# The mask of a fused attention and feed-forward kernel moved from VectorE to ScalarE, and its order planned anew

## The chip, the cores and the metric

The kernel runs on one core of a Trainium2 chip. Its engines are TensorE (PE in the rows; PEld is its loading of stationary operands), VectorE (DVE), ScalarE (ACT) and GpSimd (POOL); SyncE (SP) issues every DMA. The time is device microseconds of one execution; the figure for a kernel is the median of its runs.

## What is computed

Attention over 4 batch entries of 8 heads, 576 positions and 64 dimensions, in which each row keeps only the scores within `tau` of its largest one; then two feed-forward parts on the 2304 tokens.

```python
scores = q @ k.T / 8
thresh = max(scores, axis=-1) - tau
scores = where(scores >= thresh, scores, -1e9)
attn = exp(scores - max(scores)); attn /= sum(attn) + 1e-9
x = attn @ v                                  # to (2304, 512)
x = ((x @ w1) * (x @ w2)) @ w3 @ w_out        # 512 -> 1024 -> 1024 -> 512
h = x @ w_in; out = (h * sigmoid(h)) @ w_out2  # 512 -> 2048 -> 512
```

## The kernel before

Every float32 operand of a product is split into a high and a low part of the narrower type that TensorE takes, and a product is made of three passes (high by high, high by low, low by high). The feed-forward weights arrive as 64-bit words. For the first batch entry they are turned into float32 in SBUF, by one ScalarE instruction ("w scale", line 931) and three VectorE instructions ("w shift", "w sign", "w low", lines 938, 945 and 953), and written back to DRAM; the later entries load the float32 copy.

Attention is done in tiles of 128 query rows, 36 for a batch entry and 144 in all. For each tile (function `qtiles`) TensorE writes the scores to one of two PSUM buffers `s` (line 677). VectorE takes the row maximum, negated, into a free column of that buffer ("max", line 653), and makes two small vectors from it ("bias", lines 661 and 667): the bias of exp, and the threshold. ScalarE takes exp of the scores from PSUM into an SBUF buffer `e` (line 704). VectorE reads the scores a second time, compares them with the threshold, multiplies `e` by the result and accumulates the row sums ("mask", line 714); with it the buffer `s` is done. ScalarE scales the sums, VectorE takes the reciprocal, and the probabilities become pairs of fp16: the high part on ScalarE (line 747), the low part on VectorE (line 754) or, for some tiles, on GpSimd. A transposing DMA brings them to `pt`, and TensorE multiplies them with the values (line 818).

The program has stages. Stage 0 is the attention of the first batch entry together with the product of `w3` and `w_out` (called W34, line 1022). Each of the four stages that follow is the feed-forward part of one batch entry (line 976, function `product`, 1344 matmuls in each stage) merged with the attention of the next. All products take turns on two PSUM buffers `m`. Each one is emptied by ScalarE first (a copy at line 401, a tanh at line 1090, or half of an output at line 1113) and in most cases by VectorE after it (lines 1059 and 1097).

The order on each engine is not written by hand. `Plan` records every operation with an expected duration, and `Plan.run` makes a list schedule: at each step it takes the operation that can start first by the expected times, and among equals the one with the least priority. A priority is the place in the merged program plus a shift from the table `BIAS`, by kind of operation and phase. In the schedule before, VectorE and GpSimd do not know of each other. The schedule is made while the program is built; on the chip each engine runs its instructions in the order written.

Of the kernel before, what the change touches and what calls it, by code (L numbers as in the profile page):

```python
# [30 lines left out]
BIAS = [  # L31
    {
        "1/sum": -468, "bias": -68, "consts": 57, "exp": -44, "kh": -81, "kl": -76, "mask": -267,
        "max": 18, "p": 155, "p hi": -98, "p lo": 55, "pv": -15, "qh": -23, "qk load": -40,
        "ql": 28, "scores": -62, "sum": 3, "tau load": 69, "turn": 40, "v load": 22,
# [3 lines left out]
    },  # L39
    {  # L40
        "w low": 288, "w scale": 37, "w shift": -86, "w sign": -12, "w34": -80, "w34 keep": -68,
        "w34 out": 165, "w64 load": -100,
    },
    {
        "w low": 1206, "w scale": -64, "w shift": -69, "w sign": -25, "w34": 51, "w34 keep": -63,
        "w34 out": -84, "w64 load": -57,
    },
    {
# [7 lines left out]
    },  # L56
    {
        "1/sum": 41, "bias": -22, "exp": 14, "g": -12, "kh": -98, "kl": 30, "mask": -9, "max": 30,
        "p": -62, "p hi": -52, "p lo": 17, "product": -29, "pv": -172, "qh": 34, "qk load": -68,
        "ql": 5, "scores": -60, "split hi": 104, "split lo": -55, "sum": -24, "tanh": 8,  # L60
# [46 lines left out]
    },  # L107
    {
        "a": -22, "ab": -17, "g": -27, "o": 34, "o half": -92, "out": -97, "product": 29,
        "split hi": 21, "split lo": -20, "tanh": 88, "w hi": -36, "w lo": 38, "w load": -11,  # L110
        "y hi": -85, "y lo": -13,
    },
]
# [1156 lines left out]
```

## Time and profile before

| What | Value |
|---|---|
| Runs (3) | 1053.49, 1053.56, 1053.84 us |
| Median | 1053.56 us |
| Profiled execution, span from first to last instruction | 1052.6 us |
| Mean granted TensorE clock | 0.992 of full speed |
| Busy PE, DVE, ACT, POOL | 974.8, 678.1, 640.4, 558.1 us |
| DMA | 175.26 MB, 65.1% of 16 engines' span |

The profiled execution is known by its span; the median of the runs is 0.96 us above it. Busy time of an engine is the time in which at least one of its instructions runs. It is an average over stages that differ, so it is read by stage. The ends of matmuls are modelled, so PE's busy time holds some waiting. ACT and DVE start an instruction a little before the last one has ended; the cost of one in a dense stretch is therefore the distance from start to start.

### The profile page before, as it was taken

How to read it: one execution, taken by the hardware profiler on the slowest of the kernel's cores; microseconds unless marked ns; L12 is line 12 of the kernel's file. 1: busy time of each engine (PE TensorE's matmuls, PEld its weight loads, DVE VectorE, ACT ScalarE, POOL GpSimd, SP SyncE). 2: the span in 40 equal slices, each digit the busy share in tenths (PEclk: the TensorE clock that was granted, in tenths of full speed). 3: DMA queues.
4: the chain of work that ended last, by engine and by line, in shares of the span. 5: the costliest groups of instructions: out<-in, count | busy, mean ns of one | idle time of the engine just before them, and what ended most of it. 6: DMA issues, size and time to landing. Idle time of an engine off the chain costs nothing.

```text
span 1052.6 us, 18100 instructions
## 1 busy us (share of the span) xinstructions
PE 974.8 (93%) x6832; PEld 900.7 (86%) x6832; DVE 678.1 (64%) x1334; ACT 640.4 (61%) x980; POOL 558.1 (53%) x305
## 2 busy tenths in 40 slices
PE   3479988999888989999999999999999999999998
PEld 2345556999888888999899999999999999999998
DVE  7999899997999999873881756656477221112021
ACT  6677777777675867764774756655676523324350
POOL 3343434666384574465475673754663735646472
PEclk9989999999999999999999999999999999999999
DMA  7899989995798979856753739465466332222221
GB/s 213 211 247 242 243 193 269 278 278 129 208 254 204 264 202 249 196 134 134 161 148 106 163 114 210 138 152 134 128 121 159 102 113 92 80 81 81 81 81 66
DMA packets 213368, 175.26 MB, mean 166 GB/s; under 512 B 175264, under 2 KB 179360, under 8 KB 213280
## 3 DMA queue, kind: packets, MB, share of 16 engines
q1 hardware_dynamic: 213280, 174.10, 65.1%
q8 instruction: 54, 0.88, 0.3%
q14 instruction: 34, 0.28, 0.1%
HBM read 112.20 MB, written 19.40 MB: 125 GB/s over the span
## 4 chain that ended last, share of the span: by engine, by line
PE 55%; DVE 21%; DMA 11%; ACT 6%; issue 6%; SPq 1%; POOL 1%; ACTq 0%; DVEq 0%; POOLq 0%
PE m L976 45%; DMA pt<-hl 4%; PE m L818 4%; PE s L677 4%; DVE hl L754 3%; DVE s L653 3%; DVE e L714 2%; DVE wr L953 2%; PE m L1022 2%; DMA w<-wr 2%; DVE wr L945 2%; DMA qk<-qkv 1%; ACT hl L747 1%; DVE tb L1097 1%; DMA vr<-qkv 1%
## 5 line engine op out<-in xcount | busy, mean ns | idle before, releaser
L976 PE MATMUL m<-act,hi 128*128 128x288 f32 x2560 | 450.7, 298 | 13.5 <-DVE tb L1097 7.9
L976 PEld LDWEIGHTS m<-act,hi 128*128 128x128 f32 x2560 | 375.1, 189 | 19.4 <-DVE tb L1097 9.3
L420 POOL TENSOR_TENSOR lo<-wr,hi 128x1024 fp32r<-128x1024 f32 x102 | 249.5, 2447 | 227.5 <-PE m L976 131.3
L976 PE MATMUL m<-act,lo 128*128 128x288 f32 x1280 | 274.0, 296 | 0.0
L976 PEld LDWEIGHTS m<-act,lo 128*128 128x128 f32 x1280 | 206.0, 189 | 0.0
L401 ACT ACTIVATE hi<-wr 128x1024 fp32r<-128x1024 f32 x112 | 118.4, 1057 | 116.5 <-PE m L976 82.1
L976 PE MATMUL m<-x,hi 128*128 128x288 f32 x1024 | 179.7, 297 | 3.9 <-DVE x L847 1.2
L420 POOL TENSOR_TENSOR act<-tb,act 128x576 fp32r<-128x576 f32 x96 | 151.3, 1582 | 43.4 <-ACT act L401 28.9
L976 PEld LDWEIGHTS m<-x,hi 128*128 128x128 f32 x1024 | 150.2, 189 | 6.9 <-DVE x L847 2.1
L754 DVE SCALAR_TENSOR_TENSOR hl<-e,st,hl 128x576 f16<-128x576 f32 x117 | 126.5, 1095 | 33.4 <-ACT hl L747 33.0
L704 ACT ACTIVATE e<-s,st,sc 128x576 f32<-128x576 f32 x144 | 118.5, 826 | 46.4 <-DVE hl L754 16.2
L714 DVE SCALAR_TENSOR_TENSOR e<-s,st,e 128x576 f32<-128x576 f32 x144 | 115.5, 810 | 14.3 <-ACT e L704 12.6
L653 DVE TENSOR_REDUCE s<-s 128x1 f32<-128x576 f32 x144 | 108.0, 756 | 24.7 <-PE s L677 24.6
L677 PE MATMUL s<-kh,qs 128*128 128x288 f32 x320 | 81.6, 338 | 44.5 <-DVE e L714 25.7
L1097 DVE SCALAR_TENSOR_TENSOR tb<-ta,m 128x576 f32<-128x576 f32 x64 | 48.0, 750 | 104.0 <-ACT ta L1090 99.9
L976 PE MATMUL m<-x,lo 128*128 128x288 f32 x512 | 109.5, 295 | 0.0
L677 PEld LDWEIGHTS s<-kh,qs 128*128 128x128 f32 x320 | 54.6, 202 | 61.5 <-issue 41.2
L747 ACT ACTIVATE hl<-e,st 128x576 f16<-128x576 f32 x117 | 87.8, 768 | 28.2 <-DVE st L727 14.2
L818 PE MATMUL m<-pt,vst 128*128 128x288 f16 x656 | 99.9, 296 | 5.0 <-DMA pt<-hl 2.8
L818 PEld LDWEIGHTS <-vst 128*128 128x128 f16 x656 | 60.5, 101 | 32.3 <-issue 8.8
L420 POOL TENSOR_TENSOR qs<-qk,qs 64x576 fp32r<-64x576 f32 x31 | 49.3, 1590 | 69.9 <-ACT qs L508 55.3
L401 ACT ACTIVATE act<-tb 128x576 fp32r<-128x576 f32 x96 | 65.4, 682 | 29.9 <-DVE tb L1097 25.4
(69 smaller groups left out, 1073.5 us busy)
## 6 DMA issues: line engine op xcount, KB each, us to landing
wr<-w SPq DMA_DIRECT2D x88, 512.0 KB, 3.4
qk<-qkv SPq DMA_DIRECT2D x31, 576.0 KB, 4.8
r<-wo SPq DMA_DIRECT2D x24, 512.0 KB, 6.1
w<-wr SPq DMA_DIRECT2D x24, 512.0 KB, 4.7
vr<-qkv SPq DMA_DIRECT2D x16, 576.0 KB, 4.2
r<-w3t SPq DMA_DIRECT2D x16, 512.0 KB, 5.6
r<-w SPq DMA_DIRECT2D x16, 512.0 KB, 6.3
r<-win SPq DMA_DIRECT2D x16, 512.0 KB, 5.7
```

The costliest lines, as they stand in the source:

```text
L401: kind, n, lambda: nc.scalar.activation(out=out(), in_=a(), func=ACTF.Copy), r, w, hold, ns
L420: lambda: nc.gpsimd.tensor_tensor(out=out(), in0=a(), in1=b(), op=ALU.subtract),
L653: lambda: nc.vector.tensor_reduce(out=low(), in_=sp.t[:, :, 0:HALF], axis=AX.XY, op=ALU.max, negate=True),
L677: nc.tensor.matmul(out=sp.t[:, a, 0:HALF], lhsT=q.t[:, o:o + 128], rhs=k.t[:, a * HALF:(a + 1) * HALF], start=(n == 0), stop=(n == len(mms ...
L704: lambda n=n, sp=sp, e=e: nc.scalar.activation(out=h2(e.t), in_=sp.t[:, :, 0:HALF], func=ACTF.Exp, bias=col(1, n), scale=sc.t,),
L714: lambda n=n, sp=sp, e=e: nc.vector.scalar_tensor_tensor(out=h2(e.t), in0=sp.t[:, :, 0:HALF], scalar=col(2, n), in1=h2(e.t), op0=ALU.is_ge ...
L747: lambda: nc.scalar.activation(out=hl.t[:, 0:S], in_=e.t, func=ACTF.Copy, scale=r()),
L754: lambda: nc.vector.scalar_tensor_tensor(out=hl.t[:, S:2 * S], in0=e.t, scalar=r(), in1=hl.t[:, 0:S], op0=ALU.mult, op1=ALU.subtract,),
L818: nc.tensor.matmul(out=ps.t[:, a, 0:HALF], lhsT=v2.t[:, n, :], rhs=pt.t[:, c, a * HALF:(a + 1) * HALF], start=(first and n == 0), stop=(fi ...
L945: lambda: nc.vector.scalar_tensor_tensor(out=ri(), in0=high(), scalar=-0x80000000, in1=ri(), op0=ALU.bitwise_and, op1=ALU.bitwise_or,),
L976: nc.tensor.matmul(out=ps.t[:, a, 0:HALF], lhsT=a_.t[:, k * 128:(k + 1) * 128], rhs=x_.t[:, a * HALF:(a + 1) * HALF], start=(n == 0 and i ...
L1097: lambda: nc.vector.scalar_tensor_tensor(out=h2(g32.t), in0=h2(t.t), scalar=1.0, in1=ps.t[:, :, 0:HALF], op0=ALU.add, op1=ALU.mult,),
```

## The change

The mask goes to ScalarE. VectorE now makes one small vector per tile, minus the row maximum plus 8 tau. ScalarE adds it to the scores in PSUM, in place, by a parametric ReLU with slope 1e36 below zero (line 619 of the changed kernel), so that what lies below the threshold becomes hugely negative. Exp then reads the result with a constant bias `eb`, and its accumulator gives the row sums (line 627). VectorE's second pass over the scores (line 714 before) and one of its two small operations (line 667 before) are gone.

The schedule is made in another way: the table `BIAS`, and the phases that it was indexed by, are dropped; operations of GpSimd and the kinds of VectorE's listed in `PORT` are planned one after the other, as if they shared one resource; the expected times of the split products and of the score products have a floor of 133.4 ns for a matmul. These things change the order on every engine. The number of instructions that do the remaining work is the same.

```diff
-# into how many phases a merge is cut
-CUTS = 3, 4, 2, 1, 1
-# the priorities' shifts, by phase and kind of op
-BIAS = [
-    {
-        "1/sum": -468, "bias": -68, "consts": 57, "exp": -44, "kh": -81, "kl": -76, "mask": -267,
...
-]
+PORT = {"p lo", "w shift", "w sign", "w low", "w lo", "vl", "kl", "ql", "v scale"}
...
     def op(self, kind, eng, ns, fn, r=(), w=(), hold=(), turn=False):
...
+        o.port = eng == "POOL" or eng == "DVE" and kind in PORT
...
-        o.prio = (self.base + BIAS[min(self.phase, len(BIAS) - 1)].get(kind, 0.0), len(self.ops))
+        o.prio = (self.base, len(self.ops))
...
-                    key = (max(at, t), o.prio)
+                    key = (max(at, t, port if o.port else 0.0), o.prio)
...
-            if time(o) > start:
+            if time(o) > start + 1e-6:
...
             end = free[o.eng] = start + o.ns
+            if o.port:
+                port = end
...
-    def mm(n, width):
-        return n * (width * 0.4167 + 2.5) + 3
+    def mm(n, width, f32r=False):
+        return n * max(width * 0.4167 + 2.5, 133.4 if f32r else 0.0) + 3
...
+            nc.vector.tensor_tensor(out=eb.t, in0=sc.t, in1=tau8.t, op=ALU.mult)
...
             tiny(
                 "bias", lambda: nc.vector.tensor_tensor(
-                    out=col(1, n), in0=low(), in1=sc.t, op=ALU.mult
-                ),
-                [sp, k_m, sc], [k_b[n]],
-            )
-            tiny(
-                "bias", lambda: nc.vector.scalar_tensor_tensor(
-                    out=col(2, n), in0=low(), scalar=-1.0, in1=tau8.t, op0=ALU.mult, op1=ALU.add,
-                ),
-                [sp, k_m, tau8], [k_t[n]],
+                    out=col(1, n), in0=low(), in1=tau8.t, op=ALU.subtract
+                ),
+                [sp, k_m, tau8], [k_b[n]],
             )
...
-            plan.op(
-                "exp", "ACT", 720,
+            es.append(e)
+
+            plan.op(
+                "mask", "ACT", 640,
+                lambda n=n, sp=sp: nc.scalar.activation(
+                    out=sp.t[:, :, 0:HALF], in_=sp.t[:, :, 0:HALF], func=ACTF.Prelu,
+                    bias=col(1, n), scale=1.0, alpha=1.0e36,
+                ),
+                [k_b[n]], [sp], hold=[st],
+            )
+            plan.op(
+                "exp", "ACT", 810,
                 lambda n=n, sp=sp, e=e: nc.scalar.activation(
-                    out=h2(e.t), in_=sp.t[:, :, 0:HALF], func=ACTF.Exp, bias=col(1, n),
-                    scale=sc.t,
-                ),
-                [sp, k_b[n]], [e], hold=[st],
-            )
-            es.append(e)
-        for n, (sp, e) in enumerate(zip(sps, es)):
-            plan.op(
-                "mask", "DVE", 730,
-                lambda n=n, sp=sp, e=e: nc.vector.scalar_tensor_tensor(
-                    out=h2(e.t), in0=sp.t[:, :, 0:HALF], scalar=col(2, n), in1=h2(e.t),
-                    op0=ALU.is_ge, op1=ALU.mult, accum_out=col(4, n),
-                ),
-                [sp, e, k_t[n]], [e, k_s[n]], hold=[st],
+                    out=h2(e.t), in_=sp.t[:, :, 0:HALF], func=ACTF.Exp, bias=eb.t,
+                    scale=sc.t, accum_out=col(4, n),
+                ),
+                [sp, eb], [e, k_s[n]], hold=[st],
             )
```


Three places of the order, with buffer numbers. First ScalarE, in stage 0, at the same two tiles of the first pair of heads (buffers `s1` and `s0`, then `e1` and `e2`). Before:

```order
L704 ACTIVATE e1_392<-s1_356,st0_384,sc_130 128x576
L931 ACTIVATE act6_400<-r641_361 128x512
L931 ACTIVATE act7_403<-r641_361 128x512
L747 ACTIVATE hl0_410<-e0_351,st3_336 128x576
L704 ACTIVATE e2_419<-s0_372,st0_384,sc_130 128x576
L722 ACTIVATE st0_384<-st0_384 128x2
L508 ACTIVATE qs00_132<-qk0_405 128x576
L737 ACTIVATE e1_392<-e1_392,st0_384 128x576
L704 ACTIVATE e0_454<-s1_413,st1_450,sc_130 128x576
L401 ACTIVATE hl1_465<-e1_392 128x576
L747 ACTIVATE hl2_475<-e2_419,st0_384 128x576
```

Of the change (line 619 is the new operation, 627 exp, 650, 317 and 660 the making of the fp16 high parts, 844 "w scale"):

```order
L619 ACTIVATE s1_335<-s1_335,st0_360 128x2x288
L650 ACTIVATE e2_330<-e2_330,st3_311 128x576
L627 ACTIVATE e1_380,st0_360<-s1_335,eb_132,sc_130 128x576
L317 ACTIVATE hl2_393<-e2_330 128x576
L660 ACTIVATE hl0_397<-e0_345,st3_311 128x576
L619 ACTIVATE s0_353<-s0_353,st0_360 128x2x288
L844 ACTIVATE act5_412<-r640_292 128x512
L627 ACTIVATE e2_416,st0_360<-s0_353,eb_132,sc_130 128x576
L426 ACTIVATE qs11_136<-qk0_376 128x576
L635 ACTIVATE st0_360<-st0_360 128x2
```

Where one ScalarE instruction read a score buffer, two now do, and each exp has its own masking ahead of it on the same engine.

VectorE at the same two tiles. Before (653 "max", 661 and 667 "bias", 714 "mask", 938 to 953 the weights' words, 727 the reciprocal):

```order
L653 TENSOR_REDUCE s1_356<-s1_356 128x1
L945 SCALAR_TENSOR_TENSOR act4_354<-r640_311,act4_354 128x512
L661 TENSOR_TENSOR st0_384<-s1_356,sc_130 128x1
L667 SCALAR_TENSOR_TENSOR st0_384<-s1_356,tau8_131 128x1
L653 TENSOR_REDUCE s0_372<-s0_372 128x1
L945 SCALAR_TENSOR_TENSOR act5_363<-r640_311,act5_363 128x512
L661 TENSOR_TENSOR st0_384<-s0_372,sc_130 128x1
L667 SCALAR_TENSOR_TENSOR st0_384<-s0_372,tau8_131 128x1
L953 SCALAR_TENSOR_TENSOR act4_354<-r640_311,act4_354 128x512
L714 SCALAR_TENSOR_TENSOR e1_392,st0_384<-s1_356,st0_384,e1_392 128x576
L938 TENSOR_SCALAR act6_400<-act6_400 128x512
L938 TENSOR_SCALAR act7_403<-act7_403 128x512
```

Of the change (572 "max", 580 "bias", 667 the low part of the probabilities, 640 the reciprocal, 851 to 866 the weights' words):

```order
L572 TENSOR_REDUCE s1_335<-s1_335 128x1
L580 TENSOR_TENSOR st0_360<-s1_335,tau8_131 128x1
L851 TENSOR_SCALAR act3_351<-act3_351 128x512
L640 RECIPROCAL st3_311<-st3_311 128x2
L858 SCALAR_TENSOR_TENSOR act3_351<-r641_165,act3_351 128x512
L572 TENSOR_REDUCE s0_353<-s0_353 128x1
L866 SCALAR_TENSOR_TENSOR act3_351<-r641_165,act3_351 128x512
L580 TENSOR_TENSOR st0_360<-s0_353,tau8_131 128x1
L851 TENSOR_SCALAR act4_363<-act4_363 128x512
L858 SCALAR_TENSOR_TENSOR act4_363<-r640_292,act4_363 128x512
L572 TENSOR_REDUCE s1_401<-s1_401 128x1
L667 SCALAR_TENSOR_TENSOR hl0_397<-e0_345,st3_311,hl0_397 128x576
```

The masks are gone from between the two maxima and what follows, and words of weights and low parts stand closer behind them.

TensorE where the first product of stage 1 begins (`x0` to `x7` are the parts of the attention's output). Before, W34 (line 1022) and the scores (line 677) stand ahead of the first product (line 976):

```order
L1022 MATMUL m1_1442<-act5_363,hi1_1197 128x512
L1022 MATMUL m1_1442<-act6_400,hi1_1197 128x512
L677 MATMUL s0_1559<-kh1_1342,qs10_134 128x288 x2
L677 MATMUL s0_1559<-kl1_1348,qs10_134 128x288 x2
L1022 MATMUL m1_1442<-act7_403,hi1_1197 128x512
L976 MATMUL m0_1572<-x0_644,hi2_1345 128x288 x2
L976 MATMUL m0_1572<-x1_662,hi2_1345 128x288 x2
L976 MATMUL m0_1572<-x0_644,lo0_1376 128x288 x2
L976 MATMUL m0_1572<-x2_967,hi2_1345 128x288 x2
L976 MATMUL m0_1572<-x3_1007,hi2_1345 128x288 x2
```

Of the change (935 is W34, 469 a sum over the values, 889 the product):

```order
L935 MATMUL m1_1461<-act1_230,hi1_1278 128x512
L935 MATMUL m1_1461<-act2_281,hi1_1278 128x512
L935 MATMUL m1_1461<-act3_351,hi1_1278 128x512
L889 MATMUL m0_1490<-x0_596,hi2_1400 128x288 x2
L889 MATMUL m0_1490<-x1_600,hi2_1400 128x288 x2
L889 MATMUL m0_1490<-x0_596,lo0_1414 128x288 x2
L935 MATMUL m1_1461<-act4_363,hi1_1278 128x512
L889 MATMUL m0_1490<-x2_858,hi2_1400 128x288 x2
L889 MATMUL m0_1490<-x3_866,hi2_1400 128x288 x2
L889 MATMUL m0_1490<-x2_858,lo0_1414 128x288 x2
L935 MATMUL m1_1461<-act5_412,hi1_1278 128x512
L889 MATMUL m0_1490<-x4_1172,hi2_1400 128x288 x2
```

The last 4 of W34's 64 rows and two tiles of scores moved from ahead of the first product to behind its start: 60 rows of W34 and 184 score matmuls stand ahead of it, where 64 and 192 stood.

## Rows read from the trace of the kernel before

**Rows 1.** The page: busy time, VectorE's 40 slices, the chain that ended last
```profile
PE 974.8 (93%) x6832; PEld 900.7 (86%) x6832; DVE 678.1 (64%) x1334; ACT 640.4 (61%) x980; POOL 558.1 (53%) x305
...
DVE  7999899997999999873881756656477221112021
...
PE 55%; DVE 21%; DMA 11%; ACT 6%; issue 6%; SPq 1%; POOL 1%; ACTq 0%; DVEq 0%; POOLq 0%
```

**Rows 2.** Windows by stage: PE, PEld, DVE, ACT, POOL busy, clock, DMA share, GB/s
```profile
0.00:176.80 176.80, 130.12 (x554) 81.22 (x554) 160.55 (x366) 126.64 (x210) 66.00 (x46) 0.95 0.93 226
176.80:420.00 243.20, 225.67 (x1660) 215.71 (x1660) 226.95 (x370) 171.81 (x258) 141.11 (x73) 1.00 0.90 234
420.00:646.60 226.60, 220.43 (x1649) 213.45 (x1648) 143.87 (x315) 148.75 (x233) 130.33 (x72) 1.00 0.62 149
646.60:864.60 218.00, 215.17 (x1611) 208.45 (x1610) 121.34 (x255) 129.58 (x198) 120.80 (x65) 1.00 0.55 137
864.60:1052.60 188.00, 183.41 (x1365) 181.85 (x1363) 25.36 (x34) 63.62 (x83) 99.88 (x52) 1.00 0.24 79
```

**Rows 3.** Windows of line 976 on PE: product matmuls since the start
```profile
0.00:420.00 420.00, 191.08 (x1344) 0.98 0.91 230
...
0.00:864.60 864.60, 568.61 (x4013) 0.99 0.75 186
```

**Rows 4.** Timeline of PE around the first products: start, us, line, count
```profile
172.37 1.88 PE L1022 MATMUL m<-act,hi 128*128 128x512 f32 x4
...
176.86 0.79 PE L976 MATMUL m<-x,hi 128*128 128x288 f32 x4 [1.24 <-DVE x L847]
...
188.49 0.69 PE L976 MATMUL m<-x,hi 128*128 128x288 f32 x4
...
189.29 0.70 PE L976 MATMUL m<-x,hi 128*128 128x288 f32 x4
...
191.43 0.91 PE L818 MATMUL m<-pt,vst 128*128 128x288 f16 x6
192.08 0.78 PE L976 MATMUL m<-x,hi 128*128 128x288 f32 x4
```

**Rows 5.** Groups by line and shape: busy us, mean ns, idle before, releasers
```profile
L704 ACT ACTIVATE e<-s,st,sc 128x576 f32<-128x576 f32 x144 | 118.5, 826 | 46.4 <-DVE hl L754 16.2 <-DVE st L667 15.5 <-DVE vs L561 2.9
...
L677 PE MATMUL s<-kh,qs 128*128 128x288 f32 x320 | 81.6, 338 | 44.5 <-DVE e L714 25.7 <-DVE qs L502 5.4 <-DVE st L727 4.8
```

**Rows 6.** Timeline of DVE: start, us, line
```profile
71.62 0.81 DVE L714 SCALAR_TENSOR_TENSOR e<-s,st,e 128x576 f32<-128x576 f32 x1
...
72.35 0.81 DVE L714 SCALAR_TENSOR_TENSOR e<-s,st,e 128x576 f32<-128x576 f32 x1
...
76.22 0.14 DVE L667 SCALAR_TENSOR_TENSOR st<-s,tau 128x1 f32<-128x1 f32 x1
76.28 0.15 DVE L661 TENSOR_TENSOR st<-s,sc 128x1 f32<-128x1 f32 x1
```

**Rows 7.** Timeline of ACT, two stretches: start, us, line
```profile
10.17 0.19 ACT L542 ACTIVATION_READ_ACCUMULATOR va<-vr 128x1 f32 x1
10.27 0.81 ACT L704 ACTIVATE e<-s,st,sc 128x576 f32<-128x576 f32 x1
...
91.13 0.78 ACT L747 ACTIVATE hl<-e,st 128x576 f16<-128x576 f32 x1
91.80 0.78 ACT L737 ACTIVATE e<-e,st 128x576 f32<-128x576 f32 x1
```

**Rows 8.** Waits of PE from 177 to 420 us: total, times, longest
```profile
PE m L976 <- DVE tb L1097: 6.8, 6, 1.3
PE s L677 <- DVE e L714: 5.7, 6, 2.5
```

**Rows 9.** Two lines by themselves: min/median/max ns
```profile
L754 DVE SCALAR_TENSOR_TENSOR hl<-e,st,hl x117: 793/819/2997, 21.4 to 816.3; 128x576 f16<-128x576 f32 x117
...
L714 DVE SCALAR_TENSOR_TENSOR e<-s,st,e x144: 790/808/852, 11.3 to 812.5; 128x576 f32<-128x576 f32 x144
```

More of the change, by code (lines that the diff above doesn't have):

```diff
@@ L27 @@
 ON_DVE = {("w lo", 1): 3}
-CUTS = 3, 4, 2, 1, 1
-BIAS = [
-    {
-        "1/sum": -468, "bias": -68, "consts": 57, "exp": -44, "kh": -81, "kl": -76, "mask": -267,
-        "max": 18, "p": 155, "p hi": -98, "p lo": 55, "pv": -15, "qh": -23, "qk load": -40,
-        "ql": 28, "scores": -62, "sum": 3, "tau load": 69, "turn": 40, "v load": 22,
[3 rows of a table removed]
[L39 to L48, printed above, removed]
[7 rows of a table removed]
[L56 to L60, printed above, removed]
[4 rows of a table removed]
-    },
-    {
-        "1/sum": 34, "bias": -71, "exp": 17, "g": -38, "kh": 2, "kl": -83, "mask": 21, "max": -91,
-        "o half": -9, "p": 40, "p hi": 389, "p lo": -138, "product": 15, "pv": 36, "qh": 44,
-        "qk load": -13, "ql": -71, "scores": 15, "split hi": 16, "split lo": -45, "sum": 14,
-        "tanh": -112, "turn": -8, "v load": 71, "v scale": 247, "v sum": 49, "v total": 145,
-        "vh": -77, "vl": -77, "w hi": 180, "w keep": 69, "w lo": 45, "w low": 17, "w scale": -329,
-        "w shift": -84, "w sign": 253, "w64 load": -19, "x add": 39, "x up": -63, "xh": -40,
-        "xl": -21,
-    },
-    {
[3 rows of a table removed]
-        "split lo": 5, "sum": 39, "tanh": 11, "turn": 52, "v load": 41, "v scale": 76, "v sum": 58,
-        "v total": 51, "vh": -87, "vl": -7, "w hi": -77, "w keep": -34, "w lo": -6, "w load": -107,
-        "w low": 9, "w scale": 47, "w shift": -69, "w sign": 337, "w64 load": -5, "x add": -76,
-        "x up": -186, "xh": 15, "xl": -37,
-    },
-    {
-        "1/sum": 59, "a": -18, "ab": -4, "bias": 38, "exp": 4, "g": -82, "kh": -72, "kl": -130,
-        "mask": 82, "max": 87, "p hi": -51, "p lo": 322, "product": 72, "pv": -69, "qh": -87,
-        "qk load": 22, "ql": 38, "scores": 104, "split hi": 101, "split lo": -24, "sum": -8,
-        "tanh": 53, "turn": -54, "v load": 18, "v scale": 50, "v sum": 11, "v total": 44, "vh": 15,
-        "vl": -150, "w hi": 52, "w lo": 32, "w load": 14, "x add": -62, "x up": -37, "xh": 31,
-        "xl": -17, "y hi": -60, "y lo": -21,
-    },
-    {
[3 rows of a table removed]
-        "split lo": 50, "sum": 94, "tanh": -15, "turn": -58, "v load": 48, "v scale": -28,
-        "v sum": -62, "v total": 116, "vh": 35, "vl": -82, "w hi": -77, "w lo": 14, "w load": -37,
-        "x add": -132, "x up": 141, "xh": -44, "xl": 54,
-    },
-    {
[3 rows of a table removed]
-        "split hi": -80, "split lo": -9, "sum": 85, "tanh": -81, "turn": -83, "v load": -62,
-        "v scale": 34, "v sum": 355, "v total": -38, "vh": 50, "vl": -86, "w hi": -35, "w lo": -46,
-        "w load": 32, "x add": -58, "x up": -36, "xh": 68, "xl": 68, "y hi": 10, "y lo": -107,
[L107 to L112, printed above, removed]
-]
@@ L135 @@
         "eng", "ns", "fn", "preds", "succs", "bufs", "new", "prio", "wait", "ready", "end", "turn",
-        "psum", "kind", "phase",
+        "psum", "port",
     )
@@ L160, in __init__ @@
         self.ops, self.caps, self.queues = [], {}, {}
-        self.base, self.phase, self.stage = 0.0, 0, -1
+        self.base, self.stage = 0.0, -1
         self.window, self.busy, self.warm = 0, {}, False
@@ L225, in run @@
     def run(self):
-        free, dma = dict(self.BEGIN), 0.0
+        free, dma, port = dict(self.BEGIN), 0.0, 0.0
         head = {line: 0 for line in self.queues}
@@ L630, in qtiles @@
         k_sum, k_r = Buf(), Buf()
-        k_b, k_t = ([None] * n_t for _ in range(2))
+        k_b = [None] * n_t
         def col(row, *which):
@@ L648, in low @@
                 return sp.t[:, 1, HALF:HALF + 1]
-            k_m, k_b[n], k_t[n] = (Buf() for _ in range(3))
+            k_m, k_b[n] = Buf(), Buf()
             plan.op(
@@ L1171, in attn_steps, with merge @@
         return steps
-    def merge(a, m, lead, cuts=1):
-        phase = plan.phase
+    def merge(a, m, lead):
         plan.stage += 1
@@ L1211, in fused_kernel @@
     first = [(0.0, load_wo)] + [(5.2, lambda f=f: w34_step(f)) for f in range(8)]
-    merge(attn_steps(0), first, LEAD, CUTS[0])
+    merge(attn_steps(0), first, LEAD)
     for b in range(B):
-        merge(attn_steps(b + 1) if b + 1 < B else [], moe_steps(b), 0.0, CUTS[1 + b])
+        merge(attn_steps(b + 1) if b + 1 < B else [], moe_steps(b), 0.0)
     with tc.manual_schedule():
```

10 lines of the change are left out of this document (4 added, 6 removed), and 23 rows, old and new, of the table BIAS.

## The prediction

> **What bounds the kernel now.** I read the windows by stage first, then TensorE's own timeline, then the waits. The page says that TensorE is busy 93% of the span and that 55% of the chain that ended last is its work [rows 1]. That busy time holds waiting, so I count TensorE's work instead. Six product matmuls start 0.80 us apart (188.49 to 189.29), 0.133 us each; six of the probabilities' product start 0.65 us before what follows (191.43 to 192.08), between 0.108 and 0.133 each, and I take 0.12 [rows 4]. W34's matmuls take at most 0.47 us (four in 1.88) [rows 4].
>
> The first product of stage 1 starts at 176.86, released by VectorE's last split of the attention's output [rows 4]; 1344 products are done at 420 and all but some 19 of 4032 at 864.6 [rows 3]. So the windows are the stages [rows 2], and with the matmuls counted in the order:
>
> - Stage 0, 176.8 us: 128 x 0.47 + 192 x 0.133 + 224 x 0.12 = 113 us of work; 64 lost.
> - Stage 1, 243.2 us: 1344 x 0.133 + 164 x 0.133 + 144 x 0.12 = 218; 25 lost.
> - Stage 2, 226.6 us: with 168 score matmuls 219; 8 lost.
> - Stage 3, 218.0 us: with 116 of them 212; 6 lost.
> - Stage 4, 188.0 us: 1344 or a few more, 179 or more; at most 9 lost, the end included.
>
> All that any change of this kind can win is in these 112 us, and 89 of them lie before 420. There VectorE is the full engine: 160.6 of 176.8 us (91%) and 227.0 of 243.2 (93%), against 72% and 71% for ScalarE; from 420 on it falls to 63% and 56% [rows 2], as its slices show [rows 1]. The waits agree. TensorE's scores idled 25.7 us for the mask (L714) over the whole span [rows 5], and in stage 1 its two longest waits are for VectorE, 6.8 us for the last step that frees an accumulator (tb) and 5.7 for the mask [rows 8].
>
> **The change, part by part.**
>
> *VectorE loses* the mask and one small operation per tile. Two masks in a dense stretch start 0.73 us apart, their accumulator reads included, and the small one costs 0.06 to 0.07 [rows 6]. That is 0.80 us a tile, 115 us over 144 tiles.
>
> *ScalarE gains* the parametric ReLU and an accumulator read. No ReLU from PSUM to PSUM stands in the trace. The nearest row is a pass over 576 elements with a per-row operand, 0.67 us from start to start (91.13 to 91.80) [rows 7]; the bounds are 0.56 (if writing to PSUM saves once more the 0.11 us by which those two overlap) and 0.83, the mean duration of exp [rows 5]. I take 0.67. The accumulator read lasts 0.19, but exp starts 0.10 after it did [rows 7], so 0.10. Together 0.77 us a tile, 111 in all. The order of the change holds one load of an activation table, as before, so the ReLU brings none.
>
> The Trainium skill, page "ScalarE: Activation LUTs", section "Rules for kernel authors", speaks against such a move: simple functions like relu belong on VectorE, up to three times as fast there in bf16. For this float32 pass over PSUM the rows do not bear that out, 0.73 against 0.67 plus 0.10. By the figures in the page's section "What ACT_TABLE_LOAD costs" (280 ns and 0.833 ns per element, less 93 ns of overlap) an estimate for the new pass is 0.667 us, and the sum would be the same.
>
> *The rest of the tile.* The score buffer was released by VectorE after max, two small ones, exp and mask; now by ScalarE after max, one small one, ReLU and exp. The passes over the buffer are as many, but the step from ScalarE back to VectorE is gone, and with it the queue of weight words ahead of the mask.
>
> *Stage 0.* Ahead of the last split of the first entry's output the order has 39 ReLUs and exps where 41 exps stood, and 8 other ScalarE instructions fewer. ScalarE: 126.6 + 39 x 0.77 - 10 x 0.67 = 150 us. VectorE: 160.6 less 41 masks (29.9) and 42 small ones (2.9) is 128, and a few others are gone too. So the fullest engine goes from 161 to 150. If ScalarE is filled to the 91% that VectorE reached, the stage takes 165 us: **12 won**. Bounds: 25 (ScalarE without a gap but for some 2 us at the start) and -8 (ScalarE filled to only 81%, since it waits for VectorE and for DMA too).
>
> *Stage 1.* VectorE 227.0 - 36 x 0.80 = 198, ScalarE 171.8 + 36 x 0.77 = 200, in some 233 us 85% each. TensorE lost 25 us beside a VectorE at 93%, and 8 in stage 2 beside one at 63% and a ScalarE at 66% [rows 2]. I put 85% in the middle, 15 lost: **10 won**, bounds 17 and -5.
>
> *Moved work.* 4 W34 rows (at 0.47, 1.9 us) and 8 score matmuls (1.1) now stand behind the first product: **3 given back**.
>
> *Stage 2.* Its ScalarE, 148.8 us, gains 28 for its own tiles and about 12 more, because the order of the change brings 20 more score matmuls (5 tiles) forward into it: 189 of 227, 83%. Every accumulator is emptied by ScalarE first, so I allow **3 lost**, bounds 0 and 12. Stage 3 gets those tiles off its hands: 0. Stage 4 has hardly any attention: 0.
>
> *The table of shifts and the planned port.* They set the order only. Low parts took 793 ns at best, 819 in the middle and 2997 at worst, while the masks never took more than 852 [rows 9]: the former are held up at times, the latter not, and a schedule that knows it can put other work there. VectorE is no longer the fullest engine, so I price this at nothing; the cover is ScalarE's longer queue. Without the cover a badly ordered stage 1 costs the 10 us again.
>
> Sum: -12 - 10 + 3 + 3 = -16 against the span of 1052.6; the median of the runs is 0.96 above the span, so **1037.5 us**.
>
> **The rivals.**
>
> *ScalarE empties the accumulators late (slower).* About 105 tiles follow the first product, each with a ReLU and an exp back to back, some 1.5 us, on the engine that must free one of two accumulators while TensorE fills the other in 24 matmuls, 3.2 us. If TensorE waits x per tile for this, stage 1's win is gone and the sum is -12 + 3 + 105x. It decides from x = 0.09 us; at 0.3 the time is 1076. For it: ScalarE goes from 71% to 85% in stage 1. Against it: the waits of TensorE in stage 1 that are long are all for VectorE [rows 8], which gets quicker by what ScalarE gets slower.
>
> *DMA holds stage 0 (little gained).* The DMA share is 0.93 there, 0.90 in stage 1, at 226 and 234 GB/s [rows 2]. If the share can't pass 0.95, stage 0 needs 0.93 x 176.8 / 0.95 = 173 us and wins 4, not 12: 1045. Against it: VectorE is as full.
>
> *The lost table undoes it (no change).* The shifts may have kept the steps that free accumulators ahead of all else. If half of the 48 us that TensorE loses after stage 0 comes on top, the sum is -12 + 3 + 3 + 24 = +18; with a quarter, +6; at 6 to 9 us of it there is no change, 1053.
>
> *Both engines relieved (more gained).* With ScalarE gapless in stage 0 and stage 1 at stage 2's losses: -25 - 17 + 3 = -39, 1014.
>
> **How the numbers follow.** My forecast, 1022 to 1049, has 0.50; DMA 0.12; more gained 0.14; ScalarE late 0.12; the lost table 0.12, half of it about no change and half slower. The range from 1012 to 1060 leaves out the better end of the fourth (0.05) and the worse end of the slow ones (0.10). The runs lie within 0.35 us of each other, so 0.2% (2.1 us) is about what a measurement can tell from no change: faster 0.79, same 0.05, slower 0.16.
>
> **What would show it.** Right: the first product near 165 us; VectorE's busy time near 560 and ScalarE's near 745; the ReLU 144 times at 0.70 to 0.78 us; stage 1 near 236 us. Wrong: the first product still after 174 with the DMA share unchanged (DMA), TensorE waiting for ScalarE's copy or tanh by tens of microseconds (ScalarE late), or stages 2 and 3 longer by more than 10 us together.

## The result and the profile after

The changed kernel takes 1068.74 us (median of 4 runs, 1064.15 to 1071.77), the one before, beside it, 1053.7 (1053.49 to 1054.08). The ratio is 1.0147, 95% interval 1.0112 to 1.0182: slower by some 15 us, and outside the forecast range. The profiled execution spans 1069.9 us; it is the longest of the four, 3 us above the median.

The page of the changed kernel, with the lines that answer to [rows 1]:

```profile
PE 984.2 (92%) x6832; PEld 906.6 (85%) x6832; DVE 554.0 (52%) x903; ACT 734.1 (69%) x1268; POOL 554.3 (52%) x305
...
DVE  6777777975888777863555435335543211112021
...
PE 54%; DMA 13%; ACT 13%; DVE 10%; issue 7%; POOL 3%; SPq 0%; ACTq 0%; DVEq 0%; POOLq 0%
```

VectorE lost 124 us of busy time and ScalarE gained 94, which leaves them near the forecast 560 and 745. VectorE's share of the chain that ended last fell from 21% to 10%; ScalarE's rose from 6% to 13%. The work went where it was sent, and the time rose.

Its windows, cut at the first product and at each 1344 products (columns as in [rows 2]):

```profile
0.00:169.00 169.00, 126.35 (x539) 78.97 (x539) 122.76 (x233) 145.22 (x279) 62.68 (x45) 0.89 0.95 234
169.00:426.10 257.10, 233.72 (x1671) 220.84 (x1670) 197.28 (x262) 199.91 (x337) 138.36 (x72) 0.98 0.81 220
426.10:659.00 232.90, 226.31 (x1685) 218.69 (x1685) 127.19 (x227) 187.65 (x340) 136.91 (x76) 1.00 0.62 156
659.00:884.90 225.90, 217.70 (x1601) 209.10 (x1601) 81.85 (x150) 138.46 (x233) 117.63 (x63) 0.99 0.47 122
884.90:1069.90 185.00, 180.10 (x1345) 178.98 (x1344) 24.95 (x33) 62.89 (x82) 98.76 (x52) 1.00 0.25 83
```

The windows of [rows 2] end stages 2 and 3 a little before 2688 and 4032 products. Counted to the full numbers, the kernel before has these ends (windows of its line 976 alone):

```profile
0.00:649.00 649.00, 381.72 (x2689) 0.99 0.81 202
0.00:867.20 867.20, 571.21 (x4033) 0.99 0.74 185
```

With 176.9 and 420.0 from [rows 3, 4] that makes stages of 176.9, 243.1, 229.0, 218.2 and 185.4 us, and by the prediction's own count of work losses of about 11, 7 and 7 us in stages 2 to 4, not 8, 6 and 9. Against them the changed kernel has **-7.9, +14.0, +3.9, +7.7 and -0.4**, together +17.3 (the medians differ by 15). The stages of the experiments below are counted in the same way, each from the one profiled execution of its kernel.

TensorE's waits in stage 1, with total, times and longest, for comparison with [rows 8]:

```profile
PE m L889 <- DVE tb L1010: 4.7, 4, 1.8
PE s L590 <- ACT e L627: 4.3, 2, 3.1
PE m L889 <- DVE x L781: 4.2, 3, 1.8
PE m L889 <- ACT ta L317: 3.1, 4, 1.5
```

And the groups of the changed kernel that answer to [rows 5]:

```profile
L627 ACT ACTIVATE e<-s,eb,sc 128x576 f32<-128x576 f32 x144 | 119.3, 832 | 3.3 <-DVE hl L667 2.7
...
L619 ACT ACTIVATE s<-s,st 128x576 f32<-128x576 f32 x144 | 100.7, 708 | 16.6 <-DVE st L580 10.9 <-DVE vs L479 3.8 <-DVE vs L497 1.4
...
L590 PE MATMUL s<-kh,qs 128*128 128x288 f32 x320 | 82.5, 341 | 37.9 <-ACT e L627 31.7 <-ACT kh L434 5.9 <-issue 0.2
```

The scores' wait for the mask, 25.7 us before, has become a wait of 31.7 us for exp. Stage 1 has no one large wait; it has more kinds of them. Two stretches of its timeline show what they are (start, us, line, idle before):

```profile
191.64 3.04 DVE L667 SCALAR_TENSOR_TENSOR hl<-e,st,hl 128x576 f16<-128x576 f32 x1
191.67 2.39 POOL L336 TENSOR_TENSOR lo<-wr,hi 128x1024 fp32r<-128x1024 f32 x1 [3.02 <-PE m L889]
...
194.60 0.74 DVE L972 TENSOR_TENSOR tb<-m,ta 128x576 f32<-128x576 f32 x1
...
195.40 0.79 PE L889 MATMUL m<-x,hi 128*128 128x288 f32 x4 [1.94 <-DVE tb L972]
...
357.12 0.68 ACT L619 ACTIVATE s<-s,st 128x576 f32<-128x576 f32 x1
...
357.74 0.67 ACT L317 ACTIVATE hl<-e 128x576 f16<-128x576 f32 x1
358.31 0.62 ACT L1003 ACTIVATE ta<-m 128x576 f32<-128x576 f32 x1
358.84 0.81 ACT L627 ACTIVATE e<-s,eb,sc 128x576 f32<-128x576 f32 x1
359.56 0.18 ACT L627 ACTIVATION_READ_ACCUMULATOR e<-s,eb,sc 128x1 f32 x1
359.65 0.63 ACT L1026 ACTIVATE part<-m 128x576 f32<-128x576 f32 x1
...
359.80 0.53 PE L590 MATMUL s<-kh,qs 128*128 128x288 f32 x2 [3.12 <-ACT e L627]
```

At 191.64 a low part of the probabilities takes 3.04 us on VectorE, where 0.82 is the median, beside the low part of a weight on GpSimd that began 0.03 us later and took 2.39; `tb`, which frees an accumulator, stands behind it, and TensorE idles 1.94 us. The Trainium skill, page "SBUF — State Buffer", section "Who interferes with whom", calls the port pair that these two engines share an exclusive lock; the length of this row fits that (0.82 and 2.39 are 3.21), though the page gives the pair to whoever issues first, and here the engine with the earlier start in the trace is the one held up. At 357.12 ScalarE does a tile's ReLU, but two other instructions stand between it and the exp that releases the scores' buffer: TensorE idles 3.12 us.

### The profile page after: what moved, and what is told of

Its sections match the earlier page's. It is cut to its first block, busy times and chain, and to the rows that moved or that the text cites. A ratio compares the mean times of both kernels' runs of the same rounds, so it can differ in the third digit from the quotient of the medians.

```text
span 1069.9 us, 18028 instructions
## 1 busy us (share of the span) xinstructions
PE 984.2 (92%) x6832; PEld 906.6 (85%) x6832; DVE 554.0 (52%) x903; ACT 734.1 (69%) x1268; POOL 554.3 (52%) x305
## 4 chain that ended last, share of the span: by engine, by line
PE 54%; DMA 13%; ACT 13%; DVE 10%; issue 7%; POOL 3%; SPq 0%; ACTq 0%; DVEq 0%; POOLq 0%
PE m L889 45%; DMA pt<-hl 6%; PE m L731 5%; PE s L590 3%; ACT e L627 2%; DVE hl L667 2%; ACT hl L660 2%; ACT s L619 2%; DMA wr<-w 2%; DMA qk<-qkv 2%; POOL lo L336 1%; DMA r<-win 1%; DVE wr L866 1%; DMA r<-w 1%; ACT hi L317 1%
## 5 line engine op out<-in xcount | busy, mean ns | idle before, releaser
L889 PE MATMUL m<-x,hi 128*128 128x288 f32 x1024 | 182.3, 300 | 9.3 <-DVE tb L972 5.3
L336 POOL TENSOR_TENSOR act<-tb,act 128x576 fp32r<-128x576 f32 x96 | 147.5, 1539 | 55.2 <-ACT act L317 49.0
L667 DVE SCALAR_TENSOR_TENSOR hl<-e,st,hl 128x576 f16<-128x576 f32 x117 | 121.8, 1050 | 57.0 <-ACT hl L660 55.0
L627 ACT ACTIVATE e<-s,eb,sc 128x576 f32<-128x576 f32 x144 | 119.3, 832 | 3.3 <-DVE hl L667 2.7
L590 PE MATMUL s<-kh,qs 128*128 128x288 f32 x320 | 82.5, 341 | 37.9 <-ACT e L627 31.7
L731 PE MATMUL m<-pt,vst 128*128 128x288 f16 x656 | 104.6, 301 | 12.1 <-DMA pt<-hl 10.6
L619 ACT ACTIVATE s<-s,st 128x576 f32<-128x576 f32 x144 | 100.7, 708 | 16.6 <-DVE st L580 10.9
```

Of the source, the lines that this page charges most:

```text
L336: lambda: nc.gpsimd.tensor_tensor(out=out(), in0=a(), in1=b(), op=ALU.subtract),
L590: nc.tensor.matmul(out=sp.t[:, a, 0:HALF], lhsT=q.t[:, o:o + 128], rhs=k.t[:, a * HALF:(a + 1) * HALF], start=(n == 0), stop=(n == len(mms ...
L619: lambda n=n, sp=sp: nc.scalar.activation(out=sp.t[:, :, 0:HALF], in_=sp.t[:, :, 0:HALF], func=ACTF.Prelu, bias=col(1, n), scale=1.0, alph ...
L627: lambda n=n, sp=sp, e=e: nc.scalar.activation(out=h2(e.t), in_=sp.t[:, :, 0:HALF], func=ACTF.Exp, bias=eb.t, scale=sc.t, accum_out=col(4, n),
L667: lambda: nc.vector.scalar_tensor_tensor(out=hl.t[:, S:2 * S], in0=e.t, scalar=r(), in1=hl.t[:, 0:S], op0=ALU.mult, op1=ALU.subtract,),
L731: nc.tensor.matmul(out=ps.t[:, a, 0:HALF], lhsT=v2.t[:, n, :], rhs=pt.t[:, c, a * HALF:(a + 1) * HALF], start=(first and n == 0), stop=(fi ...
```

## The experiments

Each was timed beside the kernel before on the same chip (medians of it 1051.6 to 1054.6). Theory A in the texts on record is, in one form or another, that the new order (the lost table) is what cost and that each engine's load is worth about what the prediction put on it; Theory B, that ScalarE's longer work is itself the loss. The last two texts have a C and a D.

**Parts of the change, planned anew.**

```diff
 # kernel before, mask on ScalarE; table kept, no shared port, no floor
+ALU.subtract / Prelu / exp with accum_out, as in the change
```

> The kernel before with the mask moved to ScalarE, and nothing else: table of shifts kept, no shared port in the plan, no floor for matmuls. Theory A (the schedule lost it: without the shifts the steps that empty accumulators and feed TensorE come late, and the move of the mask gains what was forecast): about 1040 us. Theory B (the move itself loses: ScalarE's 94 us more work delay TensorE, whatever the order): 1064 to 1072 us, as the whole change.

```diff
 # kernel before
-BIAS = [ {...}, ... ]
+BIAS = [{}] * 11
```

> The kernel before with all shifts of the table zero, and nothing else. Theory A: 1070 us or more, as the loss of the table has no gain from the mask beside it. Theory B: 1052 to 1056 us, as the table does little.

```diff
 # the whole change, but
+BIAS = [ {...}, ... ]   (the table of before)
```

> The whole change, but with the table of shifts kept. Theory A: about 1040 us. Theory B: 1064 to 1072 us. If it is near 1068 while the mask alone is near 1040, the planned port or the floor is to blame and not the table.

```diff
 # the whole change, but the mask, its bias and the sums as before, on VectorE
```

> The whole change, but with the mask left on VectorE: no table, the port planned, the floor in place. Theory A: 1075 us or more. Theory B: about 1054 us.

```diff
 # the whole change without the shared port and the floor
-o.port = eng == "POOL" or eng == "DVE" and kind in PORT
-return n * max(width * 0.4167 + 2.5, 133.4 if f32r else 0.0) + 3
```

> The mask on ScalarE and the shifts zero, without the planned port and without the floor. So far dropping the table alone cost 36 us, and the mask won 25 against the same change without it. If the port and the floor do nothing: 1064 to 1072 us, as the whole change. If they do the work: 1085 us or more. If they harm: 1055 us or less.

```diff
 # kernel before
+BIAS = [{k: v / 2 for k, v in d.items()} for d in BIAS]
```

> The kernel before with each shift of the table halved. Theory A1 (the table holds a rule, such as emptying accumulators ahead of other work, that acts by sign and size): between the kernel before and the one without a table, 1055 to 1075 us. Theory A2 (the table holds no rule; it is one pick that fits this very program, and any other order is an ordinary one): 1080 to 1115 us, no better than without a table.

| Kernel | us | Ratio, 95% interval |
|---|---|---|
| mask on ScalarE under the old table | 1116.4 | 1.0614 (1.0584 to 1.0644) |
| before without a table | 1088.7 | 1.0361 (1.0318 to 1.0404) |
| the whole change with the old table | 1103.1 | 1.0491 (1.0462 to 1.0519) |
| the whole change, mask on VectorE | 1093.8 | 1.0395 (1.0362 to 1.0428) |
| mask on ScalarE, no table, no port or floor | 1089.3 | 1.0349 (1.0304 to 1.0393) |
| before, all shifts halved | 1122.2 | 1.0658 (1.0608 to 1.0708) |

The first and the third lie outside the figures of both theories, the last above both. Without its table the kernel before loses 36 us. Half a table is worse than none, and so is a table under which another program is planned: it is one pick for one program, not a rule that can be scaled or carried over. The mask's move gains 25 us in one pair (1093.8 to 1068.7) and nothing in the other (1088.7 to 1089.3). Each pair compares two orders, though, and an order alone is worth tens of microseconds. So these runs don't price the move.

**A rule in the table's place.** If the lost table had kept the steps that free accumulators ahead of all else, a shift for these alone should bring the time back.

```diff
 # the whole change
+BIAS = [{"a": -150, "ab": -150, "tanh": -150, "g": -150, "y hi": -150, "y lo": -150,
+         "o half": -150, "o": -150, "x up": -150, "x add": -150}] * 11
```

> The whole change, with one rule in place of the table: what empties an accumulator (kinds a, ab, tanh, g, y hi, y lo, o half, o, x up, x add) has a shift of -150 in every phase. Theory A1: 1045 to 1058 us, as TensorE's waits for these steps (some 16 us in stage 1) go. Theory A2: 1062 to 1080 us, no gain that stands out.

1064.6 us, 1.0109 (1.006 to 1.0158): no difference from the changed kernel that these runs can tell. This one rule does not bring back what a table gave.

**Loads added or taken at a fixed order.** Here the order stays as it is on every engine. In the changed kernel a pass is added per tile on either engine:

```diff
+for n, e in enumerate(es):
+    nc.vector.tensor_reduce(out=col(2, n), in_=e.t, axis=AX.X, op=ALU.max)   # one kernel
+    nc.scalar.activation(out=e.t, in_=e.t, func=ACTF.Copy)                   # the other
```

> The changed kernel with a maximum over e (576 elements, 0.68 us from start to start) added on VectorE for each of the 144 tiles, ahead of the reciprocal; its result is not used, and it is planned at no time, so that the order of all other instructions stays word for word. It gives VectorE 98 us back of the 115 that the mask's move took away. Theory A (the move of the mask is worth 22 us at a given order, as forecast for stages 0 and 1): 1085 to 1100 us. Theory B (VectorE is no bound in this order): 1068 to 1075 us.

> The changed kernel with a copy of e onto itself (576 elements, 0.59 us from start to start) added on ScalarE for each of the 144 tiles, ahead of the scaling of the sums, planned at no time: 85 us more on ScalarE, as much as the masking brought, at an unchanged order. Theory A (ScalarE has room): 1075 to 1085 us, as ScalarE gets fuller than it is. Theory B (ScalarE's load is what delays TensorE): 1095 us or more, more than the same load on VectorE costs.

In the kernel before the mask is left out (neither masking nor row sums are computed, a constant stands for the sum), and in another kernel the ScalarE copy is added:

```diff
-nc.vector.scalar_tensor_tensor(out=h2(e.t), in0=sp.t[:, :, 0:HALF], scalar=col(2, n), ...)
+nc.vector.tensor_scalar(out=col(4, n), in0=e.t[:, 0:1], scalar1=0.0, scalar2=576.0, ...)
```

> The kernel before with the masking left out, at an unchanged order: in its place VectorE writes a constant row sum (one small operation), so nothing is masked and nothing summed. It takes some 95 us off VectorE and frees the score buffer with exp. Theory A (VectorE's relief is worth at this order about what the same load cost at the changed one, 0.25 us per us): 1028 to 1036 us. Theory B (the order was fitted to VectorE's load, and the relief is lost in it): 1048 us or more.

> The kernel before with a copy of e onto itself added on ScalarE for each of the 144 tiles, ahead of the scaling of the sums, at an unchanged order: 85 us more on ScalarE (640 to about 725). Theory A (ScalarE, 61% busy, has room for it): 1058 to 1070 us. Theory B (it costs as at the changed kernel, 0.45 us per us, from the first): 1088 us or more, and moving the mask at this order is a loss.

| Kernel | us | Ratio, 95% interval | Against its own base |
|---|---|---|---|
| changed, more VectorE (98 us) | 1093.4 | 1.037 (1.0351 to 1.0388) | +24 |
| changed, more ScalarE (85 us) | 1106.7 | 1.051 (1.0483 to 1.0537) | +38 |
| before, mask left out | 1033.4 | 0.983 (0.9781 to 0.9879) | -19 |
| before, more ScalarE (85 us) | 1072.1 | 1.0189 (1.0148 to 1.0231) | +20 |

From start to start the added passes take 0.66 us on VectorE and 0.57 on ScalarE in these traces, 95 and 83 us in all, about what was put on them. The same copy on ScalarE costs 0.23 us per us of load in the kernel before (20 of 85), and 0.45 in the changed one (38 of 85). In the latter VectorE has been relieved, but ScalarE is fuller too (734 us busy against 640) and the order is another, so which of these doubles the price is not shown. The windows of the kernel without the mask, for stages 0 and 1, and two stretches within stage 1:

```profile
0.00:166.80 166.80, 126.64 (x555) 79.48 (x555) 139.67 (x325) 124.39 (x208) 64.59 (x45) 0.97 0.96 238
166.80:410.90 244.10, 228.02 (x1660) 218.61 (x1660) 211.29 (x330) 173.56 (x260) 145.40 (x74) 0.98 0.90 234
...
280.00:290.00 10.00, 6.06 (x33) 5.82 (x32) 7.69 (x7) 6.34 (x9) 5.66 (x4) 0.70 1.07 264
330.00:340.00 10.00, 7.91 (x49) 6.78 (x48) 6.79 (x13) 7.78 (x14) 3.22 (x4) 0.83 0.87 273
```

Here stage 0 gains 10.1 us without the masks, and stage 1 is 1.0 us longer; stages 2 to 4 gain 0.7, 2.7 and 0.1. Together that is 12.6, where the median gains 19: this execution, 1042.09 us, is the longest of its four, 8.7 above their median. Part of that lies in stage 1, in the two stretches above. In the first TensorE waits 3.94 us for a `tb` that stands behind a low part of 2.92 us on VectorE, beside the low part of a weight on GpSimd, and then runs at a lower granted clock:

```profile
282.16 2.34 POOL L420 TENSOR_TENSOR lo<-wr,hi 128x1024 fp32r<-128x1024 f32 x1 [1.64 <-PE m L975]
282.19 2.92 DVE L753 SCALAR_TENSOR_TENSOR hl<-e,st,hl 128x576 f16<-128x576 f32 x1
285.15 0.75 DVE L1096 SCALAR_TENSOR_TENSOR tb<-ta,m 128x576 f32<-128x576 f32 x1
...
285.96 1.33 PE L975 MATMUL m<-act,hi 128*128 128x288 f32 x4 [3.94 <-DVE tb L1096]
```

If all of the 8.7 us lay in stage 1, the median execution would gain near 8 there. What the masks cost in stage 1 is known no closer than that.

**Tables fitted to the program.** A search over the shifts gave new tables for the changed program (two) and for the same plan with the mask on VectorE (one).

```diff
+BIAS = [{"sum": 75, "ql": 60, "w34 keep": 684, "v scale": 84, "kl": -593, ...}, ...]
```

> The changed kernel with a new table of shifts, fitted to this very program (mask on ScalarE, shared port and floor planned); the instructions are those of the changed kernel, in another order. Theory A (the loss is the table that was fitted to the old program and lost; the mask's move itself is a gain): 1035 to 1052 us, under the kernel before. Theory B (the longer ScalarE chain per tile is what costs, whatever the order): 1060 us or more, within 10 of the changed kernel.

> The same plan (shared port and floor, a table of shifts fitted to the program) with the mask left on VectorE. Theory A: the mask's move is still worth 10 to 25 us between two fitted orders, so this one takes 1050 to 1070, above the retuned one. Theory B: at or under the retuned one with the mask on ScalarE.

> As the retuned kernel, with a second table found from another start. Theory A: within 10 us of the first retuned one, 1037 to 1058, and under the changed kernel by at least 10. Theory B: 1060 or more. If the two tables differ by more than 15 us, one table's time says little and the cause stays open by that much.

They took 1058.57 us (1.0049, 1.0029 to 1.0069), 1068.34 (1.014, 1.0103 to 1.0177) and 1074.81 (1.0173, 1.0102 to 1.0244). The first table wins 10 us back; the second, for the very same program, is no different from the changed kernel that these runs can tell (its interval covers 1.0147). None reaches the kernel before. Theory A's figure for the first was missed, and by its own condition (two tables over 15 us apart) the pair with the mask on VectorE says little.

**The mask moved, the order kept.** This holds the order fixed. In the first kernel a list holds the order of before: TensorE, GpSimd and SyncE issue the very same rows, VectorE the same without its masks and second small operations, ScalarE the same with a ReLU right ahead of each exp. The second is the mirror: the changed kernel's order, the mask back on VectorE.

```diff
-            best = None
-            for eng, c in cand.items():
...
+            o = self.ops[ORDER[done]]
+            start = max(free.get(o.eng, 0.0), time(o))
```

> The kernel before with its own order kept by a list: TensorE, GpSimd and SyncE issue what they issued, VectorE's masks and second small operations are taken out, and ScalarE's ReLU stands right ahead of each exp, whose accumulator gives the sums. So the mask's move alone, with no new plan. Theory A (the engines' times decide; the new plan is what cost): minus 19 for VectorE and plus 20 for ScalarE, 1045 to 1062 us, far under the 1116 of the same instructions planned anew under the old table. Theory B (ScalarE's longer chain per tile costs by itself): 1070 or more.

> The mirror of it: the changed kernel's order kept by a list, with the mask and its small operation put back on VectorE (where the plan has exp ended) and the ReLUs taken out of ScalarE. Theory A (what VectorE's load cost in the changed order, 24 us for 98, against what ScalarE's cost, 38 for 85): 28 more and 42 less, 1045 to 1065. Rival: the changed order lives off VectorE's relief, and the masks hold its tiles up: 1075 to 1100.

The first took 1074.7 us, 1.0205 (1.0163 to 1.0247), the second 1116.54, 1.0605 (1.0567 to 1.0643). Theory A's sum, -19 and +20, falls here: at this order the move costs 22 us, within Theory B's figure. From the kernel without the mask to this one ScalarE's passes cost some 40 (0.983 to 1.0205), about 0.4 us per us of the 104 that 144 ReLUs and accumulator reads take at 0.62 and 0.10. That is more than the 0.23 of the copy at the same order; but the copy stands ahead of the sums' scaling and the ReLU ahead of exp, on the way to the score buffer's release, so the place may count as well as VectorE's relief. The windows of the first:

```profile
0.00:180.60 180.60, 131.93 (x555) 79.62 (x555) 135.47 (x243) 155.66 (x292) 66.11 (x46) 0.96 0.89 223
180.60:425.20 244.60, 227.48 (x1660) 216.97 (x1660) 205.38 (x256) 198.95 (x332) 141.44 (x72) 0.99 0.88 232
425.20:660.90 235.70, 225.30 (x1667) 217.43 (x1665) 119.71 (x207) 177.13 (x311) 133.00 (x74) 0.99 0.58 145
660.90:887.10 226.20, 217.42 (x1613) 208.81 (x1612) 98.66 (x167) 148.98 (x255) 120.82 (x65) 1.00 0.49 130
887.10:1073.70 186.60, 180.83 (x1346) 179.28 (x1344) 24.94 (x33) 62.95 (x82) 98.52 (x52) 1.00 0.23 79
```

By stage that is +3.7, +1.5, +6.7, +8.0 and +1.2. Its waits of TensorE over the span begin with:

```profile
PE s L858 <- ACT e L895: 23.2, 23, 4.3
PE m L1157 <- DVE tb L1278: 10.2, 11, 1.5
```

Over the span the scores waited 25.7 us for VectorE's mask before [rows 5] and wait 23.2 for ScalarE's exp here: the wait changed its engine. In the profiled execution without the mask the wait for exp is 13.5, in 6 places:

```profile
PE s L677 <- ACT e L704: 13.5, 6, 4.4
```

In the mirror the scores' wait for the mask is 58.2 us:

```profile
L793 PE MATMUL s<-kh,qs 128*128 128x288 f32 x320 | 82.6, 342 | 74.7 <-DVE e L830 58.2 <-DVE st L783 9.7 <-ACT kh L632 5.8
```

Moving the mask in either direction costs, 22 and 48 us, the second beyond even the rival's 1075 to 1100. A kept order was made for where the mask stood, so each of the two holds the price of the move, with its sign, and that of an order that no longer fits. If the misfit were alike in both, it would be 35 us and the move by itself a gain of 13; nothing here separates them.

**A share of the masks.** If the move only overshoots a balance, moving some of the masks, in the stages where VectorE is full, should gain.

```diff
+def RELU(tile):
+    return tile < 36 and tile % 2 == 0   # the other kernel: tile < 72
```

> The order of before kept by a list; only every second tile of the first batch entry (18 of 144) is masked on ScalarE, the others on VectorE as before. Theory C (the engines' costs are curved, and a share of the masks moved in the stage where VectorE is full gains what moving all of them loses): VectorE's relief of 14 us in stage 0 is worth half of the 10 that leaving out all of its masks there gave, ScalarE's 12 us cost little: 1045 to 1050 us. Theory D (each ReLU ahead of an exp holds up the scores from the first one on): 1052 to 1058.

> The same for the first two batch entries: every second tile, 36 of 144. Theory C: under the one before or level with it, 1042 to 1050 us. Theory D: 1054 to 1062, a quarter of what moving all 144 cost on top of before or more.

1056.44 us, 1.0045 (1.0026 to 1.0063), and 1055.57, 1.0032 (1.0014 to 1.0051): 18 masks cost about 5 us, 36 about 4. No share that was tried gains, so Theory C's figures are missed; both times lie in D's, but not as a price per mask, since 18 more cost nothing more. These two also kept an order made for VectorE's masks.

## Why the prediction was wrong

**Right:** the prices on both engines. A ReLU in a dense stretch takes 0.62 us from start to start (357.12 to 357.74) where I took 0.67, the accumulator read adds 0.09 (359.56 to 359.65), and both busy times came out within 11 us; at the kept order VectorE's fell by only 94 us (678.1 to 584.2), as its low parts got longer there (1154 ns on the mean, 1095 before). That without the masks the first product starts at 166.8, where 165 was forecast, confirms nothing: the 165 were to be set by ScalarE.

**The step that failed: busy share taken as the measure of what a stage loses.** I set "if ScalarE is filled to the 91% that VectorE reached" for stage 0, and for stage 1 "I put 85% in the middle, 15 lost: 10 won". By stages the sum was -12, -7 (the 10, less the 3 of moved work), +3, 0 and 0; -7.9, +14.0, +3.9, +7.7 and -0.4 came.

- Stage 1 did not follow the shares. At the kept order they came out about as I had put them, VectorE 205.4 and ScalarE 199.0 of 244.6 us (84% and 81%); TensorE's order, and so its 218 us of work, is that of before, and 27 us are lost, not 15. The stage is 1.5 us longer, not 10 shorter. In the changed kernel the shares are lower still, 77% and 78%, and with 221 us of work 36 are lost. I had read a share of 93% as a limit where the longest waits, 6.8 and 5.7 us of 243 [rows 8], were small. How much VectorE's fullness alone cost there stays open, from nothing to some 8 us.
- A part of stage 1's loss is the clock: a mean granted clock of 0.98 over 257.1 us holds back at most 5 us of TensorE's full speed, where the kernel before had 1.00. The prediction has no term for it.
- Stage 0 did gain from VectorE, 10.1 us, but at the same order ScalarE's passes took back 13.8 (166.8 to 180.6), with ScalarE at 86% of the stage (155.7 of 180.6); in the changed kernel it is 86% too (145.2 of 169.0), not 91. I wrote that the step from ScalarE back to VectorE, and the queue of weight words ahead of the mask, would be gone. They are; the buffer then waits in ScalarE's queue, for exp, 23.2 us over the span.
- Stages 2 and 3 stood at +3 and 0. At the kept order they are +6.7 and +8.0, in the changed kernel +3.9 and +7.7. VectorE had slack there [rows 2], so its relief paid little for ScalarE's passes. That the 3 for stage 2 nearly came is partly luck, as the kept order, which moves no tiles into it, has more. The two stages are 11.6 us longer in the changed kernel: the last of the signs of being wrong came true. In stage 3 these 8 us lie in many waits under 2 us, and I can't name one cause.
- The two engines' terms don't add: -19 without the masks and +20 with the copies, but +22 with the mask moved, all at one order. Whether VectorE's relief, ScalarE's own load or the place of the pass makes the difference is not shown.

**The table and the planned port: "I price this at nothing".** As a sum this held better than its reason: from the kept order to the changed kernel the new plan is worth -6 us (1074.7 to 1068.7, hardly more than these runs can tell), by stages -11.6, +12.5, -2.8, -0.3 and -1.6, with the 3 of moved work in the first two. But that VectorE is no longer fullest, which I gave as the reason, is not shown to be what made it small: an order is worth tens of microseconds in either sign. Stage 1 missed its -7 by 21: 11.5 of that stand at the kept order already, and 9.5 are the new order's beyond the moved work. The prediction had named that price, "a badly ordered stage 1 costs the 10 us again", and left it out of the sum.

**The rivals.** The lost table gave the right time (+18 was its upper price, +15 came). Its mechanism, the steps that free accumulators, is not borne out: a shift for these alone changes nothing clear. That the old order was fitted and the new one is not remains a rival: with the table's very order kept the move costs 22, but that order was fitted to the mask on VectorE. ScalarE late is nearest in kind, though in the score buffers more than in the accumulators: in stage 1 TensorE waits 4.3 us for exp and 3.1 for `ta`, not tens. DMA did not hold stage 0 as that rival had it: the first product started at 169.0, before its 173, with a share of 0.95, and at 166.8 without the masks, with 0.96. That a share near these holds a shorter stage is not excluded.

**What stays open.** Eight orders with the mask on ScalarE took 1058.6 to 1116.4 us, six with all masks on VectorE 1053.6 to 1122.2. None of the former beat the kernel before. Whether some order would, these runs don't say; that the order of before is slower with its mask moved, they do. Without any fitted table the move took 1093.8 to 1068.7 in one pair and 1088.7 to 1089.3 in the other. So the 15 us are not divided here between ScalarE's passes and an order that fits less well.

## What to carry to other kernels

Before work is moved to a less busy engine, ask what stands behind that engine in its order: here every score buffer and every accumulator passes through ScalarE, and a wait of 25.7 us for VectorE became one of 23.2 for ScalarE. Don't read a stage's loss off busy shares: in stage 1 VectorE's fell from 93% to 84%, and TensorE lost no less. Test a load by taking it out at a fixed order, and look whether the profiled execution is a typical one. And price a move and a new schedule apart, but not by one kept order alone: it is fitted to where the work stood, and here the move costs at the kept order in both directions.
